# A 3136-point transform split as 49 by 64 instead of 56 by 56 in a spectral layer with a gated FFN

## The chip, the cores and the metric

The kernel runs on one core of one Trainium2 chip. A core has a matrix engine (TensorE; PE in the profile, its weight loads PEld), three engines for elementwise work (VectorE = DVE, ScalarE = ACT, GpSimd = POOL), SyncE (SP), which here issues every DMA, and 16 DMA engines between the chip's memory and the on-chip buffers (SBUF for data, PSUM for what TensorE writes). Each engine works through its own list of instructions in a fixed order and waits where an operand or a buffer isn't ready. The metric is the device time of one execution in microseconds.

## The reference

For each of 8 batches a real sequence of 3136 positions by 256 channels goes through a spectral layer and a gated FFN, all in float32:

```
X  = rfft(x, axis=1)                           # x: (8, 3136, 256)
Yr = X.real @ w_r - X.imag @ w_i + b_r         # w_r, w_i: (256, 256)
Yi = X.real @ w_i + X.imag @ w_r + b_i
Y  = shrink(Yr) + 1j * shrink(Yi)              # sign(a) * max(|a| - 0.01, 0)
y  = irfft(Y, n=3136, axis=1)
h  = relu(y @ w_in)                            # w_in: (256, 1024)
c  = sum over k of conv_w[k] * h shifted by k - 1
out = (h * sigmoid(c)) @ w_out                 # w_out: (1024, 256)
```

## The kernel before

The transform of length 3136 = 56 * 56 is done in two steps, as matmuls with constant tables, and the inverse in two steps backwards. Position s is n * 28 + j with 112 rows n and 28 columns j (`H`), where two neighbouring rows belong to one of 56 positions of the first step. The stages, for all 8 batches:

- **Stage 1** (`stage1`, L245): a unit is 4 of the 28 columns (`JC`), so 7 units a batch, 56 in all. It loads x (L236), does two matmuls with 512 columns each against the table `f1`, copies each out of PSUM on ACT (L246) into `a1`, and writes that to the scratch `sc1` of its batch in DRAM (L247). The 7 units of batch 0 are done at the start by `stage1_head` (L260, L265).
- **Stage 2** (`stage2`, L280): a step of the main loop takes one item, 4 frequencies u of the first step (`UG`) out of 28 (`U`), so 7 items a batch, 56 in all. Its operand `a2` is read from `sc1` (`load_a2`, L270); it needs all units of its batch. Eight matmuls of 128 columns; ACT and DVE take the result out as a high part `fh` and a low part `fl` (L283 to L288).
- **mix** (L304): the complex 256 by 256 product, as 36 matmuls of 256 columns with high and low parts; then bias, shrink and again a split into `sh` and `sl` on DVE, ACT and POOL (L309 to L321).
- **Stage 3** (`stage3`, L331): 12 matmuls of 256 columns for the first inverse step; ACT copies the result (L333) and a DMA writes it to the scratch `sc2` (L334).
- **Stage 4** (`stage4`, L423): a unit reads 4 of the 28 columns back from `sc2` (`z2`, L419) and does 8 matmuls of 112 columns each; 7 units a batch. ACT and DVE write the result as `yh` and `yl`, with the columns interleaved. All units of a batch are needed before its FFN begins.
- **FFN**: `up` (L442) and `down` (L470), 28 chunks of 896 positions by 8 steps. Units of stage 4 for the next batch stand between the steps.

float32 matmuls (stages 1, 2 and 4) show as two records each; the others (marked float32r) as one.

The main loop runs `for it in range(n_it + 3)`: step `it` asks for the `a2` of item it + 2, does stage 2 of item it, the mix of item it - 1 and stage 3 of item it - 3. Units of stage 1 are handed out ahead of need: `while p1 < n_it and p1 < min(it + AHEAD, NG + 2 + it + it // 2)`, one unit a step after the first few. This fixes the program's order; a scheduler with a timing model of its own then orders the instructions of each engine. Tiles get numbers in the program's order, so a higher number in a name is a later piece of the program.

Of the kernel before, what the change touches and what calls it, by code (L numbers as in the profile page):

```python
# [9 lines left out]
F32 = mybir.dt.float32  # L10
F32R = mybir.dt.float32r
# [17 lines left out]
P = 128  # L29
NT = D // P  # L30
# [3 lines left out]

def _tables():
    n = np.arange(R)
    u = np.arange(U)

    f = np.zeros((R, 2, U))
# [3 lines left out]
    f[:, 1, 0] = np.where(n % 2 == 0, 1.0, -1.0)  # L43
    fwd1 = np.zeros((2, R, U, 2, 2))
    for h in range(2):
        fwd1[h, :, :, :, h] = f.transpose(0, 2, 1)

    g = np.transpose(f, (1, 2, 0)).copy()
    g[:, 1:, :] *= 2.0
    g /= S  # L50
    inv2 = np.zeros((2, 2 * U, R, 2))
    for i in range(2):
        inv2[i, :, :, i] = g.reshape(2 * U, R)
    fwd2 = np.zeros((2, R, U, 2, SP))
    inv1 = np.zeros((2, SP, U, 2, R))
    for uu in range(U):
        for s in range(SL):
            if uu == 0:
                c = 0 if s < 29 else 1
                k = R * s if s < 29 else 28 + R * (s - 29)  # L60
                th = 2 * np.pi * ((k * n) % S) / S
                sn, cs = np.sin(th), np.cos(th)
                edge = k in (0, S // 2)
                if edge:
                    sn = np.zeros(R)
                    cs = np.round(cs)
                w = 1.0 if edge else 2.0
                fwd2[c, :, 0, 0, s] = cs
                fwd2[c, :, 0, 1, s] = -sn
                inv1[0, s, 0, c, :] = w * cs  # L70
                inv1[1, s, 0, c, :] = -w * sn
            elif s < R:
                k = uu + R * s
                th = 2 * np.pi * ((k * n) % S) / S
                sn, cs = np.sin(th), np.cos(th)
                sg = 1.0 if k <= S // 2 else -1.0
                fwd2[0, :, uu, 0, s] = cs
                fwd2[1, :, uu, 0, s] = sn
                fwd2[0, :, uu, 1, s] = -sn * sg
                fwd2[1, :, uu, 1, s] = cs * sg  # L80
                inv1[0, s, uu, 0, :] = cs
# [6 lines left out]
    return {
        "fwd1": fwd1.transpose(1, 0, 2, 3, 4).reshape(2 * R, 2 * R).astype(np.float32),
        "fwd2": fwd2.reshape(2 * R, U * 2 * SP).astype(np.float32),  # L90
        "inv1": inv1.reshape(2 * SP, U, 2, 2, H).transpose(0, 1, 4, 3, 2).reshape(2 * SP, U * 2 * R).astype(np.float32),
        "inv2": inv2.reshape(2 * R, 2 * R).astype(np.float32),
    }


# [1 line left out]
def spectral_ffn_kernel(ctx: ExitStack, tc: tile.TileContext, x, w_r, w_i, b_r, b_i,  # L97
                        w_in, conv_w, w_out, fwd1, fwd2, inv1, inv2, out):
    nc = tc.nc
    K1, K2 = 2 * R, 2 * SP  # L100
# [3 lines left out]
    sc2 = [dram.tile([K1, U, D], F32, name=f"sc2_{b}") for b in range(B)]
# [4 lines left out]
    i2 = cst.tile([K1, K1], F32, name="i2")
# [7 lines left out]
    with ExitStack() as ab:  # L117
        stg = ab.enter_context(tc.tile_pool(name="stg", bufs=1))
        wbp = ab.enter_context(tc.tile_pool(name="wbp", bufs=2))
        s1p = ab.enter_context(tc.tile_pool(name="s1p", bufs=2))  # L120
        c1 = ab.enter_context(tc.tile_pool(name="c1", bufs=1))
# [9 lines left out]
        t2 = c1.tile([K1, U, K2], F32, name="t2")  # L131
# [4 lines left out]
        inv1v = inv1.rearrange("p (u m) -> p u m", u=U)  # L136
        fwd2v = fwd2.rearrange("p (u m) -> p u m", u=U)

        def split(dst_hi, dst_lo, src):
            nc.scalar.copy(dst_hi, src)  # L140
# [3 lines left out]
            nc.sync.dma_start(f1, fwd1)  # L144

        def load_t2(g):
            nc.sync.dma_start(t2[:, g * UG:(g + 1) * UG, :], fwd2v[:, g * UG:(g + 1) * UG, :])

        def load_mix():

# [247 lines left out]
    zio, y_a = pool("zio", 3), pool("y_a")  # L398
# [6 lines left out]
    JG = 4  # L405
# [135 lines left out]
```

## Time and profile before

| | |
|---|---|
| median of 3 runs | 1770.43 us (1767.99 to 1770.92) |
| the profiled execution | 1769.05 us, its span 1767.3 us |
| mean granted TensorE clock in it | 0.995 |
| TensorE busy, share of the span | 98% |
| DVE, ACT, POOL busy | 86%, 70%, 8% |
| DMA, mean rate over the span | 93 GB/s |

The span runs from the first to the last instruction of the program; the time of the run has some 2 us around it. The page cuts the span in 40 slices of about 44 us. The transform takes the first 12 or 13 slices, with DMA busy for most of it; the FFN takes the rest, with little DMA. "Busy" counts a matmul from its start to a modelled end, and neighbours overlap, so the distance from one matmul's start to the next one's says more than the duration in a row. The chain of waits goes back from the last instruction and lists, piece by piece, what each was released by; a run of the same matmuls in it gives their time from start to start.

### The profile page before, as it was taken

Reading aid. Unit: us, or ns where it says so; the run is one execution under the profiler, and the core shown is the slowest. Engines: PE = TensorE matmul, PEld = TensorE weight load, DVE = VectorE, ACT = ScalarE, POOL = GpSimd, SP = SyncE. Lnnn points to the kernel's source line nnn. Section 1 sums busy time; section 2 is a strip of 40 time slices with the busy share of each in tenths; the row PEclk is TensorE's granted clock in tenths of the full one; section 3 lists DMA queues with packets and bytes.
Section 4 is the critical chain, followed back from the end, with each engine's and each line's share of the span. In section 5 each row is a group of like instructions: output and inputs, shape, how many; then the busy total and the mean of one; then the engine's idle time right before and its main releaser. Section 6 shows DMA issues by size and latency. Waiting matters only on the chain.

```text
span 1767.3 us, 29387 instructions
## 1 busy us (share of the span) xinstructions
PE 1731.0 (98%) x12096; PEld 1621.6 (92%) x12096; DVE 1524.3 (86%) x1820; ACT 1229.1 (70%) x1590; POOL 134.7 (8%) x60
## 2 busy tenths in 40 slices
PE   6899999999998999999999999999999999999999
PEld 2788888888998999999999999999999999999998
DVE  2899999998896988988888888888888888888887
ACT  2667777776665777777777777777777777777766
POOL 0122222222232000000000000000000000000000
PEclk8999999999999999999999999999999999999999
DMA  9777677677534110111111011111101111100001
GB/s 263 216 230 236 196 232 216 192 230 228 164 111 136 43 43 22 32 53 53 32 53 53 22 55 51 49 46 52 43 22 43 53 43 43 42 22 22 22 22 42
DMA packets 107382, 164.63 MB, mean 93 GB/s; under 512 B 8816, under 2 KB 86000, under 8 KB 107248
## 3 DMA queue, kind: packets, MB, share of 16 engines
q1 hardware_dynamic: 107248, 162.74, 30.9%
q8 instruction: 96, 1.57, 0.4%
q14 instruction: 38, 0.31, 0.1%
HBM read 85.65 MB, written 77.07 MB: 92 GB/s over the span
## 4 chain that ended last, share of the span: by engine, by line
PE 93%; DMA 3%; DVE 1%; ACT 1%; issue 0%; SPq 0%; ACTq 0%
PE acc L470 31%; PE ps_h L442 31%; PE ps_mx L304 12%; PE ps_s L423 5%; PE ps_s L280 5%; PE ps_s L331 4%; PE ps_s L245 4%; DMA i_raw<-in_inv_dram 2%; DMA z<-sc 1%; DMA sc<-ha 0%; DMA a<-sc 0%; DMA sc<-a 0%; ACT a L246 0%; DVE cw L212 0%; DVE yl L430 0%
## 5 line engine op out<-in xcount | busy, mean ns | idle before, releaser
L470 PE MATMUL acc<-wout,gh 128*128 128x256 f32 x3136 | 567.0, 280 | 0.0
L451 DVE SCALAR_TENSOR_TENSOR c<-h,cw,c 128x896 f32<-128x896 f32 x448 | 513.1, 1147 | 47.3 <-ACT c L449 46.3
L442 PE MATMUL ps_h<-yh,win 128*128 128x450 f32 x1792 | 551.0, 368 | 0.1
L470 PEld LDWEIGHTS acc<-wout,gh 128*128 128x128 f32 x3136 | 493.7, 188 | 6.5
L470 PE MATMUL acc<-wout,gl 128*128 128x256 f32 x1568 | 437.6, 281 | 0.0
L444 ACT ACTIVATE h<-ps_h 128x900 f32<-128x900 f32 x224 | 207.7, 927 | 254.8 <-PE ps_h L442 254.8
L442 PEld LDWEIGHTS ps_h<-yh,win 128*128 128x128 f32 x1792 | 338.7, 189 | 26.4 <-DVE yl L430 0.8
L442 PE MATMUL ps_h<-yl,win 128*128 128x450 f32 x896 | 329.2, 367 | 0.0
L470 PEld LDWEIGHTS acc<-wout,gl 128*128 128x128 f32 x1568 | 293.7, 188 | 0.1
L457 DVE TENSOR_TENSOR gl<-c,gh 128x896 fp32r<-128x896 f32 x224 | 243.1, 1089 | 53.6 <-ACT gh L456 50.1
L453 DVE TENSOR_TENSOR c<-h,c 128x896 f32<-128x896 f32 x224 | 243.6, 1088 | 46.9 <-ACT c L452 46.7
L456 ACT CAST gh<-c 128x896 fp32r<-128x896 f32 x224 | 209.8, 942 | 49.4 <-DVE c L453 49.4
L452 ACT ACTIVATE c<-c 128x896 f32<-128x896 f32 x224 | 213.3, 952 | 23.9 <-DVE c L451 21.0
L304 PE MATMUL ps_mx<-wmix_lo,fh 128*128 128x256 f32 x672 | 202.2, 301 | 0.0
L304 PE MATMUL ps_mx<-wmix_hi,fh 128*128 128x256 f32 x672 | 196.9, 294 | 0.5 <-DVE v L313 0.3
L304 PE MATMUL ps_mx<-wmix_hi,fl 128*128 128x256 f32 x672 | 188.7, 282 | 1.3 <-DVE fl L288 1.2
L442 PEld LDWEIGHTS ps_h<-yl,win 128*128 128x128 f32 x896 | 168.9, 189 | 11.0
L449 ACT ACTIVATE c<-h,cw 128x896 f32<-128x896 f32 x168 | 175.5, 1044 | 2.6 <-DVE gl L457 0.2
L321 POOL TENSOR_TENSOR sl<-v,sh 128x1024 fp32r<-128x1024 f32 x56 | 134.5, 2402 | 423.1 <-PE ps_s L331 300.0
L313 DVE TENSOR_TENSOR v<-ps_mx,p 64x512 f32<-64x512 f32 x224 | 154.0, 688 | 3.3
L304 PEld LDWEIGHTS ps_mx<-wmix_lo,fh 128*128 128x128 f32 x672 | 126.4, 188 | 12.3 <-issue 12.3
L304 PEld LDWEIGHTS ps_mx<-wmix_hi,fl 128*128 128x128 f32 x672 | 126.0, 188 | 11.8 <-issue 9.9
(84 smaller groups left out, 2023.0 us busy)
## 6 DMA issues: line engine op xcount, KB each, us to landing
a<-sc SPq DMA_DIRECT2D x56, 448.0 KB, 5.0
sc<-z SPq DMA_DIRECT2D x56, 448.0 KB, 3.3
z<-sc SPq DMA_DIRECT2D x56, 448.0 KB, 3.8
xr<-in_x_dram SPq DMA_DIRECT2D x55, 448.0 KB, 4.7
out_dram<-o SPq DMA_DIRECT2D x27, 896.0 KB, 4.0
sc<-a SPq DMA_DIRECT2D x49, 448.0 KB, 4.9
sc<-ha SPq DMA_DIRECT2D x7, 448.0 KB, 7.5
win_bits<-in_moe_w_in_dram SPq DMA_DIRECT2D x4, 512.0 KB, 7.6
```

The lines of the kernel that those rows point to most:

```text
L304: nc.tensor.matmul(ps[c][:, k, :], lt, rh, start=(n == 0), stop=(n == len(mm) - 1))
L313: nc.vector.tensor_tensor(v[dst, :, k, :], ps[c][src], p1[src, c], op=ALU.add)
L321: SL_ENG.tensor_tensor(sl, v, sh.bitcast(F32), op=ALU.subtract)
L442: nc.tensor.matmul(ps[:, a, 0:CH + 2], lt, rh, start=(n == 0), stop=(n == len(mm) - 1))
L444: nc.scalar.activation(h, ps[:, :, 0:CH + 2], AF.Relu)
L449: nc.scalar.mul(c, h[:, :, 0:CH], cw[:, 0, f:f + 1])
L451: nc.vector.scalar_tensor_tensor(c, h[:, :, k:k + CH], cw[:, k, f:f + 1], c, op0=ALU.mult, op1=ALU.add)
L452: nc.scalar.activation(c, c, AF.Sigmoid)
L453: nc.vector.tensor_tensor(c, h[:, :, 1:CH + 1], c, op=ALU.mult)
L456: nc.scalar.copy(gh, c)
L457: nc.vector.tensor_tensor(gl, c, gh.bitcast(F32), op=ALU.subtract)
L470: nc.tensor.matmul(acc[m // 2][:, m % 2, :], lt[:, sl], rh[:, f, :], start=(f == 0 and n == 0 and m % 2 == 0), stop=(f == NF - 1 and n == ...
```

## The change

The split becomes 49 by 64. Position s is n * 32 + j with 98 rows n and 32 columns j. Of the 49-point step the frequencies 1 to 24 are complex ("full") and frequency 0 is real. The 24 full ones make 6 items a batch (rows 0 to 95 of `sc1`); the real ones of batches 0 to 3, and of 4 to 7, make one item each, in which the four places are four batches (rows 96 and 97 of `sc1`, 64 values deep). So there are 48 + 2 = 50 items, the shared ones put ahead of the first item of batch 3 and of batch 7. Stage 1 has 8 units a batch, 64 in all; stage 4 as well. Matmuls of stage 1 have 98 rows in and out, those of stage 2 reach over 128 rows (64 for the real ones), those of stage 3 write 128 rows, those of stage 4 reach over 100 rows and have 98 columns. The pace at which units of stage 1 are handed out is four units in three steps.

```diff
-R = 56
-U = 28
-SL = 57
+R = 49
+R2 = 64
+U = 24
-H = 28
+H = 32
+NQ = H // 4
...
-    K1, K2 = 2 * R, 2 * SP
+    K1, K2, KQ, KI = 2 * R, 2 * SP, 2 * R2, 4 * (U + 1)
-    sc2 = [dram.tile([K1, U, D], F32, name=f"sc2_{b}") for b in range(B)]
+    sc2 = [dram.tile([KQ, U + 1, D], F32, name=f"sc2_{b}") for b in range(B)]
...
         def load_a2(b, g):
-            a2 = a2p.tile([K1, UG, D], F32, name="a2")
-            ld = nc.sync.dma_start(a2, sc1[b].rearrange("(u q) j d -> (q j) u d", q=4)[:, g * UG:(g + 1) * UG, :])
+            a2 = a2p.tile([KQ, UG, D], F32, name="a2")
+            if g < NG:
+                rows = slice(g * 4 * UG, (g + 1) * 4 * UG)
+                ld = nc.sync.dma_start(a2, sc1[b][rows].rearrange("(u q) j d -> (q j) u d", q=4))
+            else:
+                for k in range(UG):
+                    ld = nc.sync.dma_start(a2[0:R2, k, :], sc1[b + k][4 * U:K1].rearrange("q j d -> (q j) d"))
...
-                    nc.tensor.matmul(ps[:, k], a2[:, k, t * P:(t + 1) * P], t2[:, g * UG + k, :],
+                    rows, u = (KQ, g * UG + k) if g < NG else (R2, U)
+                    nc.tensor.matmul(ps[:, k], a2[0:rows, k, t * P:(t + 1) * P], t2[0:rows, u, :],
...
-            nc.sync.dma_start(sc2[b][:, g * UG:(g + 1) * UG, :], z1)
+            if g < NG:
+                nc.sync.dma_start(sc2[b][:, g * UG:(g + 1) * UG, :], z1)
+            else:
+                for k in range(UG):
+                    nc.sync.dma_start(sc2[b + k][:, U, :], z1[:, k, :])
...
-        AHEAD = NG + 3
         items = [(b, g) for b in range(B) for g in range(NG)]
+        for b in (0, UG):
+            items.insert(items.index((b + UG - 1, 0)), (b, NG))
         n_it = len(items)
+        firsts = [(b, jc) for b in range(B) for jc in range(NQ)]
...
-            while p1 < n_it and p1 < min(it + AHEAD, NG + 2 + it + it // 2):
-                stage1(*items[p1])
+            while p1 < min(len(firsts), NQ + 2 + 2 * it, NQ + 5 + 4 * it // 3):
+                stage1(*firsts[p1])
                 p1 += 1
...
-        z2 = zio.tile([K1, JG, D], F32, name="z2")
+        z2 = zio.tile([KI, JG, D], F32, name="z2")
```

The tables and the shapes of the other tiles follow from these numbers; the FFN is as it was.

How the order on TensorE moves is seen where a batch's first item meets the end of the batch ahead of it. Before, around the first item of batch 2: `a_1522` is the operand of item 14, `ps_s_1709` is stage 3 of item 10, `ps_s_1728` a unit of stage 1, and `ps_mx_1765` belongs to the mix of item 13, which the loop puts behind stage 2 of item 14.

```order
L331 MATMUL ps_s_1709<-sl,i_hi 112x256
L331 MATMUL ps_s_1709<-sh,i_lo 112x256
L245 MATMUL ps_s_1728<-xr,f_113 112x512
L280 MATMUL ps_s_1743<-t_114,a_1522 128x128 x4
L280 MATMUL ps_s_1752<-t_114,a_1522 128x128 x4
L304 MATMUL ps_mx_1765<-wmix_hi,fh 128x256
L304 MATMUL ps_mx_1765<-wmix_lo,fh 128x256
L304 MATMUL ps_mx_1765<-wmix_hi,fl 128x256
```

After, around the first item of batch 1: `a_644` is the operand of item 6, `ps_s_1212` is stage 3 of item 5, the last of batch 0, `ps_s_757`, `ps_s_760` and `ps_s_878` are units of stage 1, and `ps_mx_1043` is the mix of item 6 itself; `a_775` is the operand of item 7.

```order
L343 MATMUL ps_s_1212<-sl,i_hi 128x256
L343 MATMUL ps_s_1212<-sh,i_lo 128x256
L251 MATMUL ps_s_757<-xr,f_113 98x512
L251 MATMUL ps_s_760<-xr,f_113 98x512
L292 MATMUL ps_s_898<-t_114,a_644 128x128 x4
L292 MATMUL ps_s_907<-t_114,a_644 128x128 x4
L251 MATMUL ps_s_878<-xr,f_113 98x512
L316 MATMUL ps_mx_1043<-wmix_hi,fh 128x256
L316 MATMUL ps_mx_1043<-wmix_lo,fh 128x256
L316 MATMUL ps_mx_1044<-wmix_hi,fh 128x256
L316 MATMUL ps_mx_1044<-wmix_lo,fh 128x256
L292 MATMUL ps_s_1023<-t_114,a_775 128x128 x4
```

Before, the item ahead of the new batch still had its mix to do when the new batch's stage 2 came, and stage 3 was three items behind; after, mix and stage 3 of all items of the old batch stand ahead of that stage 2, and the first mix behind it is of the same item.

The same place for the shared item of batches 4 to 7 (`a_4805`, item 43), whose fourth place needs batch 7: `ps_s_5077` and `ps_s_5172` are stage 3 of items 40 and 41, and `ps_s_5003` and `ps_s_5012` the two halves of its stage 2.

```order
L343 MATMUL ps_s_5077<-sl,i_hi 128x256
L343 MATMUL ps_s_5077<-sh,i_lo 128x256
L343 MATMUL ps_s_5172<-sh,i_hi 128x256
L292 MATMUL ps_s_5003<-t_114,a_4805 128x128
L292 MATMUL ps_s_5012<-t_114,a_4805 128x128
L343 MATMUL ps_s_5172<-sl,i_hi 128x256
L343 MATMUL ps_s_5172<-sh,i_lo 128x256
L343 MATMUL ps_s_5172<-sh,i_hi 128x256
```

The other six of the item's eight matmuls stand 51 matmuls or more earlier; of the mix of item 42 nothing is left behind these rows. Between the last matmul of stage 1 of batch 7 and these two stand 10 matmuls of the mix and 13 of stage 3.

## Rows read from the trace of the kernel before

**Rows 1.** The page, its parts 1 and 2 (one digit per fortieth).

```profile
PE 1731.0 (98%) x12096; PEld 1621.6 (92%) x12096; DVE 1524.3 (86%) x1820; ACT 1229.1 (70%) x1590; POOL 134.7 (8%) x60
...
PEclk8999999999999999999999999999999999999999
```

**Rows 2.** Windows: stretch, length, busy us of each engine, PEclk, DMA share, GB/s.

```profile
0.00:40.00 40.00, 23.00 (x47) 10.21 (x48) 8.96 (x16) 8.49 (x15) 0.20 (x4) 0.84 0.94 264
40.00:100.00 60.00, 53.34 (x373) 45.22 (x371) 50.73 (x85) 36.62 (x67) 9.88 (x4) 0.99 0.76 204
150.00:500.00 350.00, 350.00 (x2633) 314.32 (x2632) 324.17 (x520) 248.42 (x397) 93.34 (x39) 1.00 0.70 207
500.00:530.00 30.00, 30.00 (x262) 30.00 (x261) 29.64 (x48) 20.61 (x32) 9.65 (x4) 1.00 0.32 95
...
550.00:555.00 5.00, 5.00 (x35) 5.00 (x35) 2.01 (x1) 2.15 (x3) 1.17 (x1) 0.74 0.02 7
555.00:575.00 20.00, 16.41 (x134) 15.51 (x134) 8.96 (x12) 10.57 (x11) 2.39 (x1) 1.00 0.88 231
600.00:1700.00 1100.00, 1100.00 (x7547) 1059.19 (x7547) 957.11 (x951) 793.29 (x927) 0.00 (x0) 1.00 0.13 40
```

**Rows 3.** Chain in order of time (start, us, what), 164:175 and 816:822.

```profile
163.83 0.86 PE ps_s L245 x2
164.69 3.04 PE ps_mx L304 x26
167.73 1.42 PE ps_s L331 x12
...
170.00 1.78 PE ps_s L280 x16
...
817.09 1.77 PE ps_s L423 x16
```

**Rows 4.** Groups by line, shapes apart: xcount, then busy us, mean ns, idle.

```profile
L304 PE MATMUL ps_mx<-wmix_lo,fh 128*128 128x256 f32 x672 | 202.2, 301 | 0.0
...
L280 PE MATMUL ps_s<-t,a 112*128 112x128 f32 x896 | 112.0, 278 | 2.7 <-DMA a<-sc 2.4 <-DMA t<-in_fwd_dram 0.3
L423 PE MATMUL ps_s<-i,z 112*128 112x112 f32 x896 | 110.3, 277 | 3.6 <-DMA z<-sc 2.7 <-DVE yl L430 0.9
...
L245 PE MATMUL ps_s<-xr,f 112*112 112x512 f32 x196 | 102.1, 602 | 16.6 <-DMA xr<-in_x_dram 10.6 <-ACT a L246 6.0
...
L331 PE MATMUL ps_s<-sh,i_hi 128*112 128x256 f32 x224 | 63.4, 283 | 2.1 <-ACT sh L320 2.1
```

**Rows 5.** Timeline (start, us, engine, line), around the last sc1 write of batch 2.

```profile
154.53 1.02 PE L245 MATMUL ps_s<-xr,f 112*112 112x512 f32 x2
...
155.59 0.59 ACT L246 COPY a<-ps_s 112x512 f32<-112x512 f32 x1 [0.27 <-PE ps_s L245]
...
156.21 0.77 SPq L247 DMA_DIRECT2D sc<-a  x1
...
160.62 0.85 SPq L270 DMA_DIRECT2D a<-sc  x2
```

**Rows 6.** Chain in order of time, 95:108, before the first item of batch 1.

```profile
99.89 3.08 DMA sc<-a
...
102.98 4.20 DMA a<-sc
```

**Rows 7.** Timeline of PE, 549:575, with idle time before and its releaser.

```profile
548.73 0.37 PE L331 MATMUL ps_s<-sh,i_hi 128*112 128x256 f32 x1 [2.12 <-ACT sh L320]
548.94 5.35 PE L423 MATMUL ps_s<-i,z 112*128 112x112 f32 x32
...
569.20 2.01 PE L423 MATMUL ps_s<-i,z 112*128 112x112 f32 x16 [1.24 <-DMA z<-sc]
```

**Rows 8.** The page, part 6: DMA issues, count, KB each, median us to landing.

```profile
a<-sc SPq DMA_DIRECT2D x56, 448.0 KB, 5.0
...
sc<-a SPq DMA_DIRECT2D x49, 448.0 KB, 4.9
```

More of the change, by code (lines that the diff above doesn't have):

```diff
@@ L36, in _tables @@
     n = np.arange(R)
-    u = np.arange(U)
-    f = np.zeros((R, 2, U))
+    n2 = np.arange(R2)
+    u = np.arange(U + 1)
+    f = np.zeros((R, 2, U + 1))
     ang = 2 * np.pi * ((n[:, None] * u[None, :]) % R) / R
@@ L42, in _tables @@
     f[:, 1, :] = -np.sin(ang)
-    f[:, 1, 0] = np.where(n % 2 == 0, 1.0, -1.0)
-    fwd1 = np.zeros((2, R, U, 2, 2))
+    fwd1 = np.zeros((R, 2, 2 * R))
     for h in range(2):
-        fwd1[h, :, :, :, h] = f.transpose(0, 2, 1)
+        for uu in range(1, U + 1):
+            for c in range(2):
+                fwd1[:, h, (uu - 1) * 4 + c * 2 + h] = f[:, c, uu]
+        fwd1[:, h, 4 * U + h] = f[:, 0, 0]
     g = np.transpose(f, (1, 2, 0)).copy()
@@ L50, in _tables @@
     g /= S
-    inv2 = np.zeros((2, 2 * U, R, 2))
+    g = np.roll(g, -1, axis=1)
+    inv2 = np.zeros((2, 2 * (U + 1), R, 2))
     for i in range(2):
[L53 to L57, printed above, removed]
+        inv2[i, :, :, i] = g.reshape(2 * (U + 1), R)
+    fwd2 = np.zeros((2, R2, U + 1, 2, SP))
+    inv1 = np.zeros((2, SP, U + 2, 2, R2))
+    for uu in range(U + 1):
+        at = (uu - 1) % (U + 1)
+        for s in range(SP):
+            k = uu + R * s
+            th = 2 * np.pi * ((k * n2) % S) / S
+            sn, cs = np.sin(th), np.cos(th)
@@ new lines, in _tables @@
+                fwd2[0, :, at, 1, s] = -sn
+                inv1[0, s, at, 0, :] = w * cs
+                inv1[1, s, at, 0, :] = -w * sn
+            else:
+                sg = 1.0 if k <= S // 2 else -1.0
+                fwd2[0, :, at, 0, s] = cs
+                fwd2[1, :, at, 0, s] = sn
+                fwd2[0, :, at, 1, s] = -sn * sg
+                fwd2[1, :, at, 1, s] = cs * sg
+                inv1[0, s, at, 0, :] = cs
+                inv1[0, s, at, 1, :] = sn
+                inv1[1, s, at, 0, :] = -sg * sn
+                inv1[1, s, at, 1, :] = sg * cs
@@ L86, in _tables @@
+    inv1[:, :, U + 1] = inv1[:, :, U]
     inv1[:, :, 1::2] = inv1[::-1, :, 1::2]
     return {
[L89 to L92, printed above, removed]
+        "fwd1": fwd1.reshape(2 * R, 2 * R).astype(np.float32),
+        "fwd2": fwd2.reshape(2 * R2, (U + 1) * 2 * SP).astype(np.float32),
+        "inv1": inv1.reshape(2 * SP, U + 2, 2, 2, H).transpose(0, 1, 4, 3, 2).reshape(2 * SP, (U + 2) * 2 * R2).astype(np.float32),
+        "inv2": inv2.reshape(4 * (U + 1), 2 * R).astype(np.float32),
@@ L99, in spectral_ffn_kernel @@
     nc = tc.nc
[L100 removed]
+    K1, K2, KQ, KI = 2 * R, 2 * SP, 2 * R2, 4 * (U + 1)
     dram = ctx.enter_context(tc.tile_pool(name="dram", bufs=1, space=DRAM))
     sc1 = [dram.tile([K1, H, D], F32, name=f"sc1_{b}") for b in range(B)]
[L104 removed]
+    sc2 = [dram.tile([KQ, U + 1, D], F32, name=f"sc2_{b}") for b in range(B)]
     cst = ctx.enter_context(tc.tile_pool(name="cst", bufs=1))
[L109 removed]
+    i2 = cst.tile([KI, 112], F32, name="i2")[:, 0:K1]
     cw = cst.tile([P, 3, NF], F32, name="cw")
@@ L130, in spectral_ffn_kernel @@
         f1 = c1.tile([K1, P], F32, name="f1")[:, 0:K1]
-        t2 = c1.tile([K1, U, K2], F32, name="t2")
+        t2 = c1.tile([KQ, U + 1, K2], F32, name="t2")
         cmx.tile([P, 96], F32, name="pad")
@@ L146, in load_t2 @@
         def load_t2(g):
-            nc.sync.dma_start(t2[:, g * UG:(g + 1) * UG, :], fwd2v[:, g * UG:(g + 1) * UG, :])
+            sl = slice(g * UG, min((g + 1) * UG, U + 1))
+            nc.sync.dma_start(t2[:, sl, :], fwd2v[:, sl, :])
         def load_mix():
@@ L165, in load_inv1 @@
         def load_inv1(g):
-            raw = stg.tile([K2, UG, K1], F32, name="i1_raw", tag="raw", bufs=2)
-            sl = slice(g * UG, (g + 1) * UG)
+            sl = slice(g * UG, min((g + 1) * UG, U + 2))
+            raw = stg.tile([K2, sl.stop - sl.start, KQ], F32, name="i1_raw", tag="raw", bufs=2)
             nc.sync.dma_start(raw, inv1v[:, sl, :])
@@ L326, in stage3 @@
             sh, sl, _ = s
-            ps = psa.tile([K1, UG, D], F32, name="ps_s3")
+            ps = psa.tile([KQ, UG, D], F32, name="ps_s3")
             for k in range(UG):
-                u = g * UG + k
+                u = g * UG + k if g < NG else U + k % 2
                 for n, (lt, rh) in enumerate(((i1_hi, sh), (i1_hi, sl), (i1_lo, sh))):
                     nc.tensor.matmul(ps[:, k, :], lt[:, u, :], rh[:, k, :], start=(n == 0), stop=(n == 2))
-            z1 = io.tile([K1, UG, D], F32, name="z1", bufs=2)
+            z1 = io.tile([KQ, UG, D], F32, name="z1", bufs=2)
             nc.scalar.copy(z1, ps)
-            nc.sync.dma_start(sc2[b][:, g * UG:(g + 1) * UG, :], z1)
+            if g < NG:
+                nc.sync.dma_start(sc2[b][:, g * UG:(g + 1) * UG, :], z1)
+            else:
+                for k in range(UG):
+                    nc.sync.dma_start(sc2[b + k][:, U, :], z1[:, k, :])
         nc.vector.memset(mlam, -LAM)
@@ L348, in spectral_ffn_kernel @@
             xh = []
-            for p in range(NG):
+            for p in range(NQ):
                 xr, ld = load_x(hx, 0, p, parts=2 if p == 0 else 1, tag=f"hx{p}")
@@ L368, in spectral_ffn_kernel @@
         wk.tile([P, 72], F32, name="pad", bufs=1)
-        i1_hi = cab.tile([K2, U, K1], F32R, name="i1_hi")
-        i1_lo = cab.tile([K2, U, K1], F32R, name="i1_lo")
+        i1_hi = cab.tile([K2, U + 2, KQ], F32R, name="i1_hi")
+        i1_lo = cab.tile([K2, U + 2, KQ], F32R, name="i1_lo")
         background = later()
@@ L385, in spectral_ffn_kernel @@
                 stage3(*items[it - 3], ss.pop(it - 3))
-            while p1 < n_it and p1 < min(it + AHEAD, NG + 2 + it + it // 2):
-                stage1(*items[p1])
+            while p1 < min(len(firsts), NQ + 2 + 2 * it, NQ + 5 + 4 * it // 3):
+                stage1(*firsts[p1])
                 p1 += 1
```

35 lines of the change are left out of this document (9 added, 26 removed).

## Prediction

> **What bounds the kernel now.** I read the page first: TensorE is busy for 98% of the span at full clock in nearly every slice [rows 1]. Then the windows: from 150 to 500 us and from 600 to 1700 us TensorE is busy without a gap, while DVE has 324.17 of 350 us and 957.11 of 1100, ACT less, and the DMA engines 0.70 and 0.13 [rows 2]. So in both long stretches a change is worth what it changes in TensorE's own work, as long as nothing makes TensorE wait. It does wait at the start (23.00 of 40 us busy, DMA share 0.94), a little up to 100 us, and where transform and FFN meet (16.41 of 20 us) [rows 2].
>
> The chain of waits gives prices from start to start: 0.86 us for a matmul of stage 1, 3.04 / 26 = 0.117 for one of the mix, 1.42 / 12 = 0.118 for one of stage 3, 1.78 / 16 = 0.111 for a record of stage 2 and 1.77 / 16 = 0.111 for a record of stage 4 [rows 3]. The counts are in the grouped lines: 896 records each in stages 2 and 4, 3 * 672 in the mix, 3 * 224 in stage 3, 196 in stage 1 outside the head [rows 4].
>
> **TensorE's work.** Items go from 56 to 50: stage 2 loses 96 records (10.7 us), the mix 216 matmuls (25.3), stage 3 72 (8.5). Stage 1 gains 8 units, 16 matmuls at 0.86 (13.8); their 512 columns are unchanged. Stage 4 gains 8 units of 8 matmuls, 128 records. Their price: stage 2 with 128 columns and stage 4 with 112 take the same 0.111 us with weights of 128 columns in both, so I take 0.111 for 98 columns too (14.2 us). If time followed columns below 112, the 1024 new records would cost 1024 * 0.111 * 98 / 112 = 99.5 us against 99.5 now, so 0. The sum is -44.5 + 13.8 + 14.2 = -16.5 us. Stage 3 writing 128 rows costs nothing: the mix does so at 0.117.
>
> Other engines: an item now takes 2 * 0.86 + 36 * 0.117 + 1.42 + 1.78 = 9.1 us of TensorE, so DVE does its 324.17 us in 350 / 9.1 = 38 items, 8.5 us each, so 6 items fewer take 51 us off it, more than TensorE loses in the transform. In the FFN the eight units more have the same 64 * 784 = 56 * 896 elements in a row, under a TensorE without gaps.
>
> **The waits that the change adds.** The first item of a batch needs the batch's last unit of stage 1: copy on ACT, write to `sc1`, read of `a2`. In the timeline that unit's matmul starts at 154.53, so it ends at 155.39; ACT begins at 155.59, the write is asked for at 156.21, the read at 160.62 [rows 5]; with 4.20 us for a read [rows 6] that is 160.62 + 4.20 - 155.39 = 9.4 us. With a write of 3.08 us [rows 6] it is 8.1; with the page's medians of 4.9 and 5.0 [rows 8] 10.7. What TensorE has to do meanwhile is counted in the order at the prices above. Before: 9.7 us for batch 1, 14.5 us for batches 2 to 6, 11.9 for batch 7, so nothing waits, as the windows show. After: batch 1 has 24 matmuls of stage 3 and 4 of stage 1, 24 * 0.118 + 4 * 0.86 = 6.3 us. Batches 2 to 6 have 7.4, 5.5, 9.2, 5.8 and 5.7. Batch 7, with the shared item, has 10 * 0.117 + 13 * 0.118 = 2.7. Behind the waiting stage 2 all of TensorE is queued, and DVE, ACT and POOL have no item left either, since the old batch's mix and most of its stage 3 are done by then.
>
> The wait is 9.4 us less the cover: 3.1 + 2.0 + 3.9 + 0.2 + 3.6 + 3.7 + 6.7 = 23.2 us. With 8.1 it is 15.2, with 10.7 it is 32.3. I take 23.2, since the timeline's case is the middle of steady running. The units of stage 1 of the next batch that the order puts into these holes are counted as work above.
>
> Two follow-up costs. After a wait of 2.12 us TensorE's granted clock fell to its lower level, 1.2 of 2.4 GHz, for part of the next 5 us (0.74), and 32 records of stage 4 took 5.35 us instead of 32 * 0.111 = 3.55 [rows 2, 7]: 1.8 us; a wait of 1.24 us at 569.20 cost nothing of the kind [rows 7, 2]. Five of the seven waits are over 3 us, but they may be cut into pieces by matmuls of stage 1: 0 to 9 us, I take 6. And the pipeline has to fill again: from 40 to 100 us, after an empty start, TensorE lost 60 - 53.34 = 6.7 us [rows 2], other waits among it. Five times 0 to 3 us, I take 4 in all.
>
> **Head and seam.** The head moves one unit more through a DMA system that is 0.94 busy, some 1 to 3 us; I take 2, and 0 if 98 rows go as fast as their bytes. At the seam one more unit of `z2` waits, 1.24 us at most where TensorE waited for one [rows 7]; I take 1, with 0 to 8 as bounds, since no row has a transfer of 100 rows.
>
> **The sum.** -16.5 + 23.2 + 6 + 4 + 2 + 1 = +19.7 us on the profiled execution's 1769.05 us is 1788.8. The median of the runs is 1.4 us above that execution, so 1790. With every low end it is -16.5 - 14.2 + 15.2 = -15.5 (1755), with every high end -16.5 + 32.3 + 9 + 15 + 3 + 8 = +50.8 (1821).
>
> **Rivals.**
> - *The holes are covered*, and only TensorE's work counts: 1770.4 - 16.5 + 3 = 1757, faster. For it: no gap in 350 us now, and DVE has slack to gain. The place is the seven joints between batches, and the point from which it decides is the time from stage 1 to a landed `a2`: at 7.6 us the seven waits still sum to 12.2 us and the gain is gone, at 5.7 only batch 7 waits. Against it: the shortest pieces of the rows give 8.1.
> - *Short waits without a price behind them*: 8.1 us each time, full clock, no refilling: -16.5 + 15.2 + 3 = +1.7, so 1772. For it: the 1.24 us wait that left the clock alone.
> - *Stage 4 gets cheaper with fewer columns*: 14.2 us off, 1776. Against it: 112 and 128 columns cost the same.
> - *Transfers of 98 and 100 rows use fewer DMA engines.* 112 rows are 7 for each of 16 engines. If 100 rows ran as 10 rows on each of 10 engines, `z2` would take 10 / 7 of the time on these; at the seam, where the share is 0.88 [rows 2], that makes DMA the bound and the 20 us some 25: +5. If 98 rows ran as 7 on each of 14 engines, a transfer of stage 1 would take as long as now, with 64 instead of 56 of them; over a period the engines used go from 0.70 to about 0.81, which doesn't bind but brings the joints to 10.7 us: 32.3 - 23.2 = +9. So 1804. The Trainium skill states such a rule ("DMA: Bandwidth & Descriptors", section "Why a DMA increments its semaphore by 16 and not by 1": the largest number up to 16 that divides the slowest dimension). By that rule 98 rows get 14 engines and 100 rows 10; no run here shows a transfer of such a size, so the trace neither bears it out nor excludes it.
>
> **Numbers.** Forecast 0.50, fewer DMA engines 0.20, short waits 0.12, holes covered 0.10, cheaper stage 4 0.08. A measurement of this kernel tells 0.2% (3.5 us) from no change. Faster takes the covered holes, 0.10; within 0.2% most of the short waits, 0.10; slower the rest, 0.80. The range from 1767 to 1809 us leaves out the covered holes and the upper part of the DMA case, under 0.2.
>
> **What would show it.** In the profile after, the window table of the transform has seven dips of TensorE some 60 us apart, the waits name `a<-sc` or the read behind `sc<-a` as releaser, and PEclk falls near the larger ones; the deepest comes with the second shared item. Stage 4's 1024 records keep 0.111 us apart, the mix 0.117. The FFN has no gap and is some 14 us longer. The prediction is wrong if TensorE runs through the joints, if its work isn't 16 us less, or if a fresh bound (DMA share near 1 throughout) shows between them.

## The result, and the profile after

The changed kernel takes 1797.12 us (median, 1792.45 to 1799.14) against 1770.68 us (1767.99 to 1772.71) for the kernel before in the same rounds: a ratio of 1.0147, 95% interval [1.0122, 1.0171]. The forecast was 1790 us. The profiled execution after has a span of 1796.0 us, 28.7 us more than before.

The page after, its parts 1 and 2:

```profile
PE 1743.9 (97%) x11872; PEld 1614.8 (90%) x11872; DVE 1501.2 (84%) x1757; ACT 1209.7 (67%) x1565; POOL 120.0 (7%) x54
...
PE   6989999998998999999999999999999999999999
...
PEclk8989999999998899999999999999999999999999
```

Against [rows 1] there are 224 fewer PE records. Counted from 1, PE now dips in slices 3 and 10 as well as at the transform's end, and its clock in slices 3, 13 and 14; slice 3 (90 to 135 us) holds the joint to batch 1. The windows after, in the columns of [rows 2]:

```profile
0.00:40.00 40.00, 22.88 (x44) 8.81 (x45) 8.44 (x15) 8.29 (x15) 0.20 (x4) 0.83 0.85 268
...
150.00:500.00 350.00, 332.12 (x2300) 282.31 (x2300) 306.31 (x459) 227.14 (x361) 81.55 (x34) 0.98 0.63 204
...
555.00:575.00 20.00, 16.81 (x118) 16.47 (x118) 9.75 (x12) 11.23 (x11) 4.72 (x2) 0.83 0.47 151
600.00:1700.00 1100.00, 1100.00 (x7575) 1059.48 (x7574) 948.27 (x950) 785.83 (x923) 0.00 (x0) 1.00 0.13 41
```

The FFN is as full as before. The transform isn't: 332 of 350 us busy, with DVE and DMA less busy than in [rows 2], so neither has become the bound there. The groups of PE after, and a row of stage 4 from the chain of waits:

```profile
L441 PE MATMUL ps_s<-i,z 100*128 100x98 f32 x1024 | 131.2, 285 | 1.4 <-DMA z<-sc 1.4
L251 PE MATMUL ps_s<-xr,f 98*98 98x512 f32 x224 | 121.2, 623 | 11.1 <-DMA xr<-in_x_dram 8.7 <-ACT a L252 2.3
L292 PE MATMUL ps_s<-t,a 128*128 128x128 f32 x768 | 103.4, 286 | 8.6 <-DMA a<-sc 8.2 <-issue 0.4
```

```profile
757.44 1.76 PE ps_s L441 x16
```

**How the loss is counted.** Busy time hides small gaps, so I count what TensorE did: each record in a stretch at its usual distance from start to start (0.430 us for a stage-1 record, of which a matmul has two, 0.112 stage 2, 0.117 mix, 0.118 stage 3, 0.112 stage 4, 0.205 and 0.117 in the FFN). The rest of the stretch is "lost". Over the span before has 1713.6 us of work and 53.7 lost, after 1697.2 and 98.9: 16.4 us less work, 45.2 us more lost.

**Table 1.** Medians, ratios to the kernel before in the same rounds, TensorE's lost time by stretch, and by how much DVE's operations were longer in sum than the median of their kind (those over 0.3 us longer), all from the profiled executions. The stretches are fixed times. In the kernels that gain, the transform ends up to 46 us earlier than after, so for them the column 120–530 holds part of the way into the FFN (the seam). Of the eight large `tensor_scalar` at L192 four are stretched after, so that their median is 0.94 us instead of 0.43 and the 24.0 is some 2 us short.

| kernel | us | ratio [95%] | 40–120 | 120–530 | 530–620 | DVE stretched |
|---|---|---|---|---|---|---|
| before | 1770.7 | | 10.8 | -0.2 | 11.2 | 5.8 |
| after | 1797.1 | 1.0147 [1.0122, 1.0171] | 16.8 | 33.4 | 17.9 | 24.0 |
| a2_old | 1763.9 | 0.9965 [0.9951, 0.9980] | 6.7 | 17.4 | 13.9 | 26.0 |
| sl_memset | 1781.5 | 1.0065 [1.0051, 1.0079] | 10.7 | 22.5 | 15.7 | 0.5 |
| both_out | 1747.8 | 0.9881 [0.9865, 0.9896] | 4.2 | 9.2 | 7.5 | 0.7 |
| sl_dve | 1777.8 | 1.0040 [1.0026, 1.0054] | 8.0 | 23.1 | 19.2 | 0 |
| s1_two | 1821.9 | 1.0293 [1.0280, 1.0307] | 9.5 | 56.4 | 27.6 | 10.9 |
| share | 1769.8 | 1.0007 [0.9997, 1.0017] | 8.9 | 20.4 | 13.0 | 19.6 |
| share_slm | 1765.7 | 0.9981 [0.9971, 0.9990] | 8.9 | 17.5 | 10.6 | 1.3 |
| share_fl | 1756.5 | 0.9925 [0.9908, 0.9941] | 9.8 | 10.4 | 11.8 | 6.6 |
| share_slm_fl | 1756.9 | 0.9920 [0.9906, 0.9935] | 9.4 | 10.6 | 10.1 | 4.8 |
| z2_split | 1799.0 | 1.0172 [1.0156, 1.0187] | 17.1 | 30.6 | 21.7 | 23.3 |
| b_share | 1782.7 | 1.0076 [1.0063, 1.0089] | 14.1 | 10.2 | 12.8 | 21.3 |
| b_fl | 1766.7 | 0.9987 [0.9978, 0.9996] | 9.3 | 0.2 | 8.3 | 5.9 |

**Where it is lost.** The waits of PE after, 40 to 600 us (us in total, times, longest):

```profile
PE ps_s L292 <- DMA a<-sc: 7.5, 5, 2.6
PE ps_s L343 <- ACT z L345: 6.6, 4, 3.4
PE ps_mx L316 <- DVE fl L300: 3.6, 4, 1.6
PE ps_mx L316 <- DVE v L325: 3.1, 2, 2.1
```

Only 7.5 us are put down to `a2`. At a joint TensorE is held several times over by what runs in it, so **Table 2** takes each joint whole: from the end of the last stage-1 matmul of a batch to the stage-2 matmul that needs it (at batches 3 and 7 the fourth place of the shared item), and the work between.

| batch | 1 | 2 | 3 | 4 | 5 | 6 | 7 |
|---|---|---|---|---|---|---|---|
| us between | 15.6 | 10.2 | 7.2 | 9.7 | 11.6 | 8.8 | 5.8 |
| work in it | 6.3 | 7.4 | 5.5 | 9.2 | 5.8 | 5.7 | 2.7 |
| lost | 9.4 | 2.8 | 1.7 | 0.4 | 5.8 | 3.1 | 3.1 |
| forecast wait | 3.1 | 2.0 | 3.9 | 0.2 | 3.6 | 3.7 | 6.7 |

The sum is 26.3 us. Not all of it was added by the change: at batch 1 the kernel before already spends 12.8 us on 9.7 of work and loses 3.1, which is the chain of [rows 6]; the prediction had "nothing waits" there. So 23.2 us were added, as many as were forecast, but joint by joint it differs. At batch 1 the read was asked for late and took 6.64 us instead of the 4.20 of [rows 6]; the chain of waits there:

```profile
104.60 2.37 DVE cw_e L194
...
107.27 0.36 SPq L180
...
108.20 6.64 DMA a<-sc
...
114.88 3.34 PE ps_s L292 x16
```

The `cw_e` row is a piece of 128x8 that normally takes 0.16 us. L180 is a load of weights that has to wait for such pieces, and SyncE, in order, asks for `a2` only behind it. The same thing is seen whole at batch 5; first the chain, then POOL's timeline:

```profile
352.92 2.37 DVE fl L300
...
360.79 2.35 DVE wout_e L192
...
363.16 0.02 ACT wout_e L193
...
363.70 1.00 ACT z L345
...
364.75 0.58 PE ps_s L343
```

```profile
352.35 2.39 POOL L333 TENSOR_TENSOR sl<-v,sh 128x1024 fp32r<-128x1024 f32 x1 [6.77 <-PE ps_s L343]
360.51 2.34 POOL L333 TENSOR_TENSOR sl<-v,sh 128x1024 fp32r<-128x1024 f32 x1 [5.76 <-PE ps_s L343]
```

An operation of 0.69 us on DVE and one of 0.43 take 2.37 and 2.35 us, and the second is through 0.29 us after POOL's `sl` (360.51 + 2.34 = 362.85 against 363.14). ACT, in order, stands behind it with the copy of `z1` that stage 3 needs, and TensorE waits 3.4 us. All 18 stretched DVE operations of the run, 24.0 us in excess, lie beside POOL's `sl`.

Behind the waits the granted clock falls: between 40 and 530 us it is at its lower level in six stretches, 27 us in sum, which costs some 14 us; before there is none. Two places, in the joint of batch 5 and behind that of batch 7:

```profile
365.00:370.00 5.00, 5.00 (x17) 3.72 (x18) 3.01 (x5) 2.27 (x4) 0.00 (x0) 0.50 1.03 347
500.00:505.00 5.00, 5.00 (x30) 4.88 (x29) 2.83 (x5) 4.00 (x7) 2.21 (x1) 0.66 0.96 322
```

So there are two theories. **A**: the joints lack cover. **B**: GpSimd's `sl` holds VectorE, and that chain is what TensorE waits for.

### The profile page after: what moved, and what is told of

Its sections match the earlier page's. It is cut to its first block, busy times and chain, and to the rows that moved or that the text cites. A ratio compares the mean times of both kernels' runs of the same rounds, so it can differ in the third digit from the quotient of the medians.

```text
span 1796.0 us, 28781 instructions
## 1 busy us (share of the span) xinstructions
PE 1743.9 (97%) x11872; PEld 1614.8 (90%) x11872; DVE 1501.2 (84%) x1757; ACT 1209.7 (67%) x1565; POOL 120.0 (7%) x54
## 4 chain that ended last, share of the span: by engine, by line
PE 83%; DVE 8%; DMA 3%; issue 3%; ACT 2%; SPq 1%; DVEq 0%; ACTq 0%
PE ps_h L460 31%; PE acc L488 31%; PE ps_s L441 6%; PE ps_mx L316 6%; PE ps_s L292 3%; PE ps_s L251 3%; DVE v L325 3%; PE ps_s L343 2%; DVE fl L300 1%; DVE fl L298 1%; DMA a<-sc 1%; DVE p L321 1%; DMA i_raw<-in_inv_dram 1%; DVE v L331 1%; DMA sc<-a 1%
## 5 line engine op out<-in xcount | busy, mean ns | idle before, releaser
L316 PE MATMUL ps_mx<-wmix_hi,fh 128*128 128x256 f32 x600 | 181.0, 303 | 4.5 <-DVE v L325 3.1
L316 PE MATMUL ps_mx<-wmix_hi,fl 128*128 128x256 f32 x600 | 173.7, 294 | 3.7 <-DVE fl L300 3.6
L316 PE MATMUL ps_mx<-wmix_lo,fh 128*128 128x256 f32 x600 | 174.5, 292 | 0.0
L333 POOL TENSOR_TENSOR sl<-v,sh 128x1024 fp32r<-128x1024 f32 x50 | 119.8, 2396 | 447.9 <-ACT sh L332 261.6
L325 DVE TENSOR_TENSOR v<-ps_mx,p 64x512 f32<-64x512 f32 x200 | 137.4, 687 | 2.9
L441 PEld LDWEIGHTS ps_s<-i,z 100*128 100x128 f32 x1024 | 131.5, 203 | 3.5 <-issue 1.8
L441 PE MATMUL ps_s<-i,z 100*128 100x98 f32 x1024 | 131.2, 285 | 1.4 <-DMA z<-sc 1.4
```

The costliest lines, as they stand in the source:

```text
L316: nc.tensor.matmul(ps[c][:, k, :], lt, rh, start=(n == 0), stop=(n == len(mm) - 1))
L325: nc.vector.tensor_tensor(v[dst, :, k, :], ps[c][src], p1[src, c], op=ALU.add)
L441: nc.tensor.matmul(ps[:, t, j * K1:(j + 1) * K1], z2[:, j, t * P:(t + 1) * P], i2, start=(j == 0), stop=(j == JG - 1), skip_group_check=True)
```

## The experiments

**The two causes apart.** `a2_old` lets each batch read the scratch of the batch before, so its output is another; `sl_memset` writes zeros instead of subtracting; `both_out` does both.

```diff
-ld = nc.sync.dma_start(a2, sc1[b][rows]...)
+ld = nc.sync.dma_start(a2, sc1[max(b - 1, 0)][rows]...)
-SL_ENG.tensor_tensor(sl, v, sh.bitcast(F32), op=ALU.subtract)
+SL_ENG.memset(sl.bitcast(F32), 0.0)
```

> The changed kernel, but every a2 load of batches 1 to 7 (and the shared item's) reads the scratch of the batch before its own, so that no stage 2 waits for the stage-1 units that have just run; the output is another for that reason, the work and the transfers are of the same number and size. Theory A (short cover: at a joint between batches the last stage-1 unit of the next batch, its store and the a2 load take 9.4 us, and too little other TensorE work lies between): the waits at the joints go, with the half clock behind them, about 39 us: 1758 us, and TensorE loses under 8 us between 120 and 530 us of the span. Theory B (the joints are only where it shows: VectorE's operations with two operands in SBUF are held while GpSimd's sl runs, 24 us in the changed kernel, and that chain is what TensorE waits for): the loss stays, 1785 us or more. Theory A with part B: 1758 to 1775, with waits left that the chain gives to VectorE.

> The changed kernel, but GpSimd's sl is a memset to zero instead of the subtraction v - sh, so that GpSimd reads nothing from SBUF; the low part of stage 3's right operand is left out by it. The order of TensorE stays about the same: the covers of the seven joints are 6.3, 7.4, 8.0, 9.1, 7.4, 5.8 and 7.1 us against 6.3, 7.4, 5.5, 9.2, 5.8, 5.7 and 2.7. Theory A: the waits at the joints fall only by the longer covers, from 23 to 15 us, with half clock and refill 1784 to 1790 us. Theory B: VectorE's 24 us of stretched operations go, TensorE waits for nothing of that chain any more: 1765 to 1775 us, with a2 the only wait left at a joint.

> Both edits that leave work out at once: a2 of batches 1 to 7 reads the batch before, and GpSimd's sl is a memset. Alone they took 33 and 16 us off. If the two causes are separate and each is seen whole in its run: 1797 - 33 - 16 = 1748 us. If the joint waits and the hold are mostly one cost counted twice (the hold stretches the chain that is exposed at a joint): 1758 to 1764 us.

`a2_old` came to 1763.9 us, 33.2 off, near theory A's 1758, inside its range with part of B, and far from B's 1785, with the stretching still there (26.0 us). `sl_memset` came to 1781.5, 15.6 off: more than A allowed, less than B. `both_out` came to 1747.8; if the two add up it is 1797.1 - 33.2 - 15.6 = 1748.3. So both theories hold, each for its part, and their effects add up.

Each edit moved something else as well. In `a2_old` the scheduler, with nothing to wait for, put stage 1 later: the last unit of a batch now begins 11 to 58 us behind the stage 2 that used to need it, so that units lie between the mixes until the end of the transform. From the first to the last stage 2 of batch 7, where they are a filler that after lacks, after loses only 1.8 us and `a2_old` none; so this explains few of the 33 us. The rest is the joints with what they bring behind them, the clock for one, and the run doesn't part these. In `sl_memset` the work at the joints grew by 3 us, their loss fell from 26 to 17, and TensorE's own waits for `sl` went (2.0 us after). That leaves room for a few us of its 15.6 by longer cover. But between `a2_old` and `both_out`, where no joint waits, the same edit takes off 16.1, so `sl` costs that much by itself; GpSimd's shorter work (0.95 us instead of 2.4) is counted in. The row of the operation most often held, after and then in `sl_memset`:

```profile
L300 DVE TENSOR_TENSOR fl<-d,fh 128x512 fp32r<-128x512 f32 x50 | 46.6, 933 | 4.3 <-ACT fh L299 3.3
```

```profile
L300 DVE TENSOR_TENSOR fl<-d,fh 128x512 fp32r<-128x512 f32 x50 | 34.4, 688 | 9.9 <-ACT fh L299 9.1
```

With both out TensorE's waits are few, and its loss from 40 to 620 us is at the level of before (20.8 against 21.8 us):

```profile
PE ps_s L251 <- ACT a L252: 2.0, 1, 2.0
PE ps_s L441 <- DMA z<-sc: 1.8, 2, 1.1
PE ps_s L343 <- ACT z L345: 1.1, 1, 1.1
PE ps_s L292 <- DMA a<-sc: 0.9, 1, 0.9
```

That is the split's own worth with the waits away, 21 us less than before: the 16.4 us of work, and about 2 us less lost in sum (51.6 against 53.7), the remaining 2 to 3 being the distance of these profiled executions from the medians.

**Taking `sl` off GpSimd with nothing left out.**

```diff
-DB, XRB, SL_ENG = 1, 3, nc.gpsimd
+DB, XRB, SL_ENG = 1, 3, nc.vector
```

> The changed kernel with sl on VectorE instead of GpSimd. It ends GpSimd's hold, and the order on TensorE comes out with covers of 5.3, 9.1, 17, 16, 19, 20 and 24 us at the joints. VectorE gets 50 x about 1.1 us more and loses about 22 us of stretching: its share of 150 to 500 us goes from 88 to about 93%. Theory A: waits only at the first joint (4 us) and none from the third on: 1760 to 1765 us. Theory B: the same direction, since the hold goes as well: 1760 to 1770 us. If VectorE then sets the pace of an item (8.3 + 1.1 us against 9.7 us of TensorE work, close together), it takes part of that back: up to 1790 us.

1777.8 us: no stretching, but the gain stops where stage 1 has run out of units. From 250 to 400 us TensorE lost 1.2 us, from 400 to 530 it lost 16.3, with DVE 128 of 130 us busy:

```profile
250.00:400.00 150.00, 149.95 (x1059) 128.06 (x1058) 148.18 (x228) 108.38 (x173) 0.00 (x0) 1.00 0.71 233
400.00:530.00 130.00, 121.98 (x917) 110.48 (x916) 128.10 (x196) 80.95 (x126) 0.00 (x0) 0.99 0.43 143
```

So the third case of the expectation came: VectorE takes part of it back as the bound.

**Giving the joints cover.** Stage 1 has one PSUM buffer, which each half unit holds until ACT has copied it out; the two runs here take this to be what keeps its units back. Handing them out earlier in the program was not tried. `s1_two` gives stage 1 a second one and stage 2 one less; `share` lets the two take from three in turn.

```diff
-ps1 = ... tile_pool(name="ps1", bufs=1, space=PSUM)
-ps2 = ... tile_pool(name="ps2", bufs=2, space=PSUM)
+ps1 = ... bufs=2   and   ps2 = ... bufs=1          # s1_two
+ps1 = ... bufs=3, both stages with tag="ps12"      # share
```

> The changed kernel with two PSUM buffers for stage 1 and one for stage 2 instead of one and two. In the order on TensorE stage 1 then runs batches ahead: over 25 us of other work lie between the last unit of a batch and the stage 2 that reads it, at every joint; GpSimd's sl stays as it is. Theory A: all joint waits go: 1758 us, plus what a single stage-2 buffer costs (the mix of the item before lies between its two halves, so little), so 1755 to 1768 us. Theory B: VectorE's stretching stays at 20 us or more and TensorE goes on waiting for it: 1780 us or more.

> The changed kernel with nothing left out: stage 1 and stage 2 take their PSUM buffers in turn from one set of three instead of one and two of their own. In the order on TensorE stage 1 then keeps about half a batch to a batch ahead: 17 to over 25 us of other work between the last unit of a batch and the stage 2 that reads it, at all seven joints, and units remain as filler between the mixes until item 40 of 50 (the run with one buffer for stage 2 had none left after item 23 and lost 25 us by it). sl stays on GpSimd. Theory A (short cover): no wait for a2 is left at a joint, TensorE loses under 20 us between 40 and 530 us of the span instead of 50, about 1764 us, as the run that read the batch before. Theory B (GpSimd's hold on VectorE): VectorE's stretched operations stay, 1775 us or more. What can take some back: the last ten items run without stage-1 units between them, 7.4 us of TensorE work against 8.3 us on VectorE, up to 9 us.

`s1_two` went the other way: 1821.9 us, 25 slower. Its waits from 120 to 530 us and a window of it:

```profile
PE ps_mx L316 <- DVE v L325: 11.7, 19, 1.2
PE ps_s L343 <- POOL sl L333: 5.6, 7, 0.8
PE ps_s L292 <- issue: 3.6, 20, 0.2
```

```profile
400.00:530.00 130.00, 113.64 (x854) 103.93 (x853) 111.35 (x172) 73.08 (x110) 33.14 (x14) 0.99 0.33 113
```

No wait for `a2` is left, so the cover did what A says of it. But with the last unit gone before item 23, no stage-1 unit lies between one mix and the next any more, and mixes wait, 19 times, for the PSUM that DVE is still reading (`v`, L325). Of the 74 us that TensorE loses from 40 us to its last stage 2, 61 lie behind the last stage-1 unit (at 309 us). Some of it may be stage 2's single buffer; the run doesn't part the two. `share` keeps units until item 40: 1769.8 us, 27 less than after, again with no wait for `a2`, which is A with nothing left out. It is 6 us above `a2_old`; the stretching stays at 19.6 us.

**Both, with nothing left out.** `share_slm` is `share` with `sl` on VectorE for items 0 to 40. `share_fl` is `share` with another operation moved, the one that was held most; `share_slm_fl` has both.

```diff
-nc.vector.tensor_tensor(fl[:, :, 2], d, fh[:, :, 2].bitcast(F32), op=ALU.subtract)
+nc.gpsimd.tensor_tensor(fl[:, :, 2], d, fh[:, :, 2].bitcast(F32), op=ALU.subtract)
```

> The shared three PSUM buffers, and sl on VectorE for items 0 to 40 and on GpSimd for the last nine, where no stage-1 units lie between the mixes. If the joint waits and the hold both cost TensorE time and VectorE (8.3 + 1.1 us an item against 9.7 us of TensorE work) just keeps up, as it did from 250 to 400 us in the run with sl on VectorE (1.2 us lost there): 1752 to 1760 us, faster than both kernels. If VectorE becomes the bound in the front part, where stage 1's units come fewer than 1.3 to an item, or the hold costs nothing once cover is there: no better than the run with sl on GpSimd throughout, or slower, 1762 to 1775 us.

> The shared three PSUM buffers, sl on GpSimd, and the third low part of stage 2's result (fl <- d - fh, 128x512, both operands in SBUF) moved from VectorE to GpSimd as well. Where the hold is what is left of the loss (120 to 530 us: 20 us lost with the shared buffers, 9 us where GpSimd read nothing): VectorE loses 50 x 0.69 us of work and the operation that was held most often, so the loss falls by up to 10 us, 1757 to 1762 us, faster than both kernels. The other way: GpSimd now works 2.4 + about 1.2 us an item and holds the operations left with two SBUF operands (min with r, 1.22 us, and the weight pieces) more often, and the mix, whose first products use that low part, waits for it: 1770 us or more.

> The shared buffers, sl on VectorE for items 0 to 40, and the third low part on GpSimd throughout. VectorE per item: 8.3 + 1.1 - 0.7 = 8.7 us against 9.7 us of TensorE work, so it keeps up with room; GpSimd works 1.2 us an item instead of 2.4 and can hold it only half as long. If holds still cost: 1755 to 1762 us, better than without the move (1766). If the gain of sl on VectorE was all that could be had in the front part and the loss is in the last ten items and the seam: 1763 to 1767 us.

`share_slm` came to 1765.7 us, above the hoped-for 1752 to 1760: from 120 to 250 us it lost only 0.3, from 400 to 530 it lost 15.0. `share_fl` came to 1756.5, ratio 0.9925 [0.9908, 0.9941], faster than both kernels, and `share_slm_fl` to the same. Windows of `share`, then of `share_fl`:

```profile
400.00:530.00 130.00, 121.88 (x963) 113.68 (x963) 124.89 (x191) 85.83 (x130) 33.87 (x16) 1.00 0.43 143
```

```profile
400.00:530.00 130.00, 126.97 (x1017) 120.71 (x1016) 111.83 (x175) 87.27 (x130) 57.52 (x30) 0.98 0.46 152
```

In the stretch where stage 1 runs out DVE goes from 125 to 112 us and TensorE does 54 records more. As `share_fl` is 8 us ahead there, its window holds less of the transform; from the last stage-1 unit to the last stage 2, `share` loses 4.1 us and `share_fl` 0.6. The stretching falls from 19.6 to 6.6 us. POOL works more, and nothing waits for it. How much of the 13 us is the hold and how much DVE's lighter load, these two runs don't part.

**Controls on the kernel before.**

> The kernel before (56 by 56) with the shared three PSUM buffers. TensorE lost nothing there from 120 to 530 us, so there is no wait for cover to remove: 1765 to 1773 us, no change. If the shared buffers had won by something other than the cover of the joints (evacuation order, the stage-2 buffers), the kernel before would gain by it too: 1745 to 1760 us.

> The kernel before (56 by 56, its own PSUM buffers) with the third low part of stage 2's result on GpSimd instead of VectorE, a control for the fastest version of the new split (1756 us). TensorE lost nothing from 120 to 530 us there, so a freer VectorE has only the start and the seam to win at: 1762 to 1771 us, and the new split with its two edits stays ahead. If the move is a gain by itself, whatever the split, this run comes to 1756 us or less, and the split adds nothing.

`b_share` is 12 us slower, not the same: the shared buffers have a price of their own, which the joints' cover outweighed in the new split. Where it lies isn't shown. The stretching of DVE rises from 5.8 to 21.3 us, so it may be the hold again, in another order of the same operations. TensorE's waits, 40 to 600 us, are for DVE at the mixes, as in `s1_two`, and once for ACT:

```profile
PE ps_mx L303 <- DVE v L312: 4.8, 5, 1.8
PE ps_s L279 <- ACT a L245: 4.0, 1, 4.0
PE ps_mx L303 <- DVE p L308: 2.9, 3, 1.4
```

`b_fl` is at 0.9987 [0.9978, 0.9996], 2 to 3 us off. The new split with its two edits stays 10 us ahead of the old one with the edit that suits it. The old one with both edits was not run.

**The seam.**

```diff
-nc.sync.dma_start(z2, zv)
+nc.sync.dma_start(z2[0:96], zv[0:96])
+nc.sync.dma_start(z2[96:KI], zv[96:KI])
```

> The changed kernel with each z2 load issued as rows 0 to 95 and rows 96 to 99. One theory of the 6.6 us more that the seam takes (530 to 600 us): a 100-row transfer shows a DMA share of 0.67 while it runs alone, where the 112-row one of before shows 1.0, so ten of the 16 engines carry it, it lands later, and TensorE's short waits for z2 with the half clock after them (576 to 593 us) follow from it. By that the waits for z2 shrink and the run is 3 to 6 us faster: 1791 to 1794 us. The rival: the loads at the seam are late because their last z1 stores are late; then nothing changes, 1795 to 1799 us, or it is slower by the cost of twice as many descriptors' issues.

No gain: 1799.0 us, and 21.7 us lost at the seam against 17.9. The share of the DMA engines during a `z2` load that runs alone, before (112 rows) and after (100 rows), half microseconds each:

```profile
742.50:743.00 0.50, 0.50 (x7) 0.50 (x6) 0.50 (x2) 0.50 (x1) 0.00 (x0) 1.00 0.96 342
743.00:743.50 0.50, 0.50 (x4) 0.47 (x4) 0.50 (x1) 0.48 (x1) 0.00 (x0) 1.00 1.02 299
```

```profile
761.50:762.00 0.50, 0.50 (x5) 0.46 (x4) 0.50 (x1) 0.45 (x1) 0.00 (x0) 1.00 0.67 240
762.00:762.50 0.50, 0.50 (x4) 0.47 (x3) 0.50 (x2) 0.05 (x1) 0.00 (x0) 1.00 0.69 227
```

The 100 rows do go by fewer engines, but the seam doesn't wait for that. What it pays is seen in PE's timeline and one window after:

```profile
573.75 5.28 PE L441 MATMUL ps_s<-i,z 100*128 100x98 f32 x32 [1.07 <-DMA z<-sc]
579.38 10.53 PE L441 MATMUL ps_s<-i,z 100*128 100x98 f32 x48 [0.35 <-DMA z<-sc]
```

```profile
580.00:585.00 5.00, 5.00 (x25) 5.00 (x25) 1.88 (x2) 1.07 (x2) 0.00 (x0) 0.50 0.46 111
```

The 48 records take 10.53 / 48 = 0.219 us each, twice the usual, with the granted clock at its lower level; they alone cost 5.2 us. The clock is there from 559 to 566 and from 576 to 593 us, in the kernel before for 3.4 us in the whole seam. `both_out` reaches the seam 46 us earlier, so its 7.5 us in Table 1 can't be set against the others. From the last record of the mix to 620 us the loss is 9.2 us before, 15.5 after, 14.3 in `both_out` and 16.8 in `share_fl`: the seam keeps its price when the transform is no longer late. What in it costs more than before is open.

## Why the prediction was right, point by point

- **What bounds it.** Right: TensorE without a gap in the long stretches, so that its work and its waits are all that counts.
- **TensorE's work, -16.5 us.** Measured -16.4. Stage 4 with 98 columns takes 1.76 / 16 = 0.110 us a record, so the rival that made it cheaper falls, and the mix stays at 0.117.
- **Waits at the joints, +23.2 us.** Right in place and in sum (26.3 less the 3.1 that batch 1 lost before), but the sum is luck: single joints are off by up to 3.6. The step that failed in size is the one latency of 9.4 us for all joints: it came to 15.6 us at batch 1 and 11.6 at batch 5, where DVE was held, and to 5.8 at batch 7, where the shared item's fourth place needs only a transfer of 64 x 256. The deepest joint was to be the last and was the first. Taking the need for `a2` away gave 33 us, with the clock behind the joints in it.
- **Clock and refilling, +6 and +4.** From 40 to 530 us the loss grew by (16.8 + 33.4) - (10.8 - 0.2) = 39.6 us, so 39.6 - 23.2 = 16.4 lie outside what the joints added, where 10 were forecast. The clock costs some 14 us in all, where 6 were forecast and 9 at most; about 6 of them lie inside the joints of Table 2, so some 8 of the 16.4 are the clock and 8 are refilling and other waits, for which 4 were forecast. A cause is missing too: the prediction gave DVE slack to gain, and nothing in it speaks of POOL holding DVE, which costs some 16 us by `sl_memset` and `both_out`, inside the joints and outside.
- **Head +2, seam +1.** Measured -0.6 and +6.7 (inside its bounds of 0 to 8). The seam was priced by one wait and not by the clock behind it.
- **The sum.** +19.7 forecast, +28.7 between the two spans: 6.4 of the difference (39.6 against 33.2) are joints, clock and refilling, 5.7 the seam, less 2.6 at the head; what is left is under 1 us.
- **The rivals.** Covered holes: didn't happen. With cover alone it is 1769.8 (`share`) or 1763.9 (`a2_old`); the 1757 worked out for it is reached only where VectorE is freer as well (`share_fl`, 1756.5). Short waits without a price: excluded. Fewer DMA engines: the mechanism is there, and its price isn't. By the Trainium skill ("DMA: Bandwidth & Descriptors", section "Why a DMA increments its semaphore by 16 and not by 1") 100 rows go by 10 engines; the trace, with a share of 0.67 to 0.69, agrees that it is well under 16. The loads of x alone at the start show 0.88 from 3 to 4 us with 98 rows and 1.10 before with 112. Yet the time didn't fall when the 96 rows were sent apart from the other four.

## What to carry to other kernels

A change that takes work off the bound engine can be paid back where a software pipeline has a dependency that jumps a whole batch: count in the order how much other work lies between producer and consumer there, and look for the single buffer (here stage 1's one in PSUM) that keeps the producer from running ahead. Run ahead no further than that, since the same units are the filler that hides the next engine's latency. And when a chain names an operation that takes several times its usual length, look at what the neighbouring engine runs in that moment, before blaming the operation.

## What the runs showed of the hardware

- A VectorE operation with both inputs in SBUF (128x512, 0.69 us) takes up to 2.76 us beside GpSimd's subtraction of SBUF operands; beside GpSimd's memset none of the 20 that overlapped it was stretched (`sl_memset`). The Trainium skill says this ("SBUF — State Buffer", section "Who interferes with whom": two SBUF inputs contend with a GpSimd instruction that reads SBUF, not with one that only writes it), and the trace agrees on both halves.
- An int32 `tensor_scalar` (0.43 us), which has one input in SBUF, was held as well, up to 2.52 us, and beside the memset too: one took 1.14 instead of 0.42 us in `both_out`.
- Who begins first decides. After, all 18 stretched operations began while `sl` was running, and each ended just behind it: 0.55 us behind for the 128x512 ones with two inputs, 1.08 for 128x1024, 0.28 for the large `tensor_scalar`, so they did their work when `sl` was through. None of the five two-input operations that began before an `sl` and overlapped it was held, nor of the ten in the kernel before.
- So the same `sl`, 2.4 us an item, stretched DVE by 5.8 us in the kernel before and by 24.0 after. Of the 5.8 only 1.3 fall between 120 and 530 us, where TensorE lost nothing.
- The granted clock stayed at 0.50 from 576 to 593 us, after one wait of 1.07 us and with one of 0.35 inside; before, one of 1.24 us left it alone [rows 7].
